# Other product orders in an exact-product feed-forward kernel, and five weight signs on another engine

## The chip, the cores and the metric

The kernel runs on one core of one Trainium2 chip. The time is the device time of one execution in microseconds (us). The engines that matter are TensorE (PE, its weight loads PEld), VectorE (DVE), ScalarE (ACT) and the DMA queue of SyncE (SP).

## What is computed

Attention within chunks of 64 positions, and then a feed-forward layer with a rational activation on its output. The inputs are 8 x 8 heads of 576 positions of 64 elements (float32); the two weight matrices come as float64.

```
scores = q_c @ k_c^T / 8                # per chunk of 64
attn   = exp(scores - max) / (sum + 1e-9)
x      = (attn @ v_c) as (4608, 512)
h = x @ w_in                            # (4608, 2048)
P = a0 + a1 h + a2 h^2 + a3 h^3
Q = 1 + |b0| |h| + |b1| h^2
out = (P / (Q + 1e-6)) @ w_out          # (4608, 512)
```

## The kernel before

**Products in parts.** A float32 product is made from three faster ones of a reduced type. Each operand is split into a high and a low part (`xhi`, `xlo`, `wi_hi`, `wi_lo`, `wo_hi`, `wo_lo`, `ghi`, `glo`), and hi x hi, hi x lo and lo x hi are added up in PSUM.

**Blocks and steps.** The 4608 tokens are 18 blocks of 256 (`NB`, `BT`), and the 2048 middle columns are four stages of 512 (`NST`). A step g is one block n and one stage s. `ff1` (L318) writes `ph`, two PSUM banks that hold 4 groups `fi` of 128 middle columns by 256 tokens: for each `fi` 4 input chunks `cc` times 3 products, 48 matmuls of 256 columns in a step, in two parts (`F`, `f`). Weights are the stationary operand and tokens the moving one. Then a chain of 12 elementwise operations (`chain_a` to `chain_glo`, L331 to L378) on ACT and DVE makes `ghi` and `glo`. `ff2` (L381) adds into `po` (two banks of 512 output columns, `i` for each half of 128 tokens): parts `Z` and `z` use `ghi` with `wo_hi` and `wo_lo`, part `y` uses `glo` with `wo_hi`. Here the tokens are stationary and the output columns moving. A product is 256 columns wide, two (`c`) for each pair of operands, except the four of a block that open and close its sums in the two banks, which are 512 wide (L390 to L392). `ff2` runs two steps behind `ff1` (`LAG`).

**Order of the work.** Nothing is scheduled by a tool. The ramp is a list written out by hand (`START`, L33): each letter is one function and the number its step, block or piece. From step 12 (block 3) on a loop (L464) issues for each step `F f`, the chain and `Z z y` of the step two before, with the attention of the next block between them: scores (`pss`) in stage 0, transposes (`pst`) in stage 1, attention times v (`psx`) in stage 2. The engines run in the order of this text, and semaphores hold an instruction until what it needs is there.

**Weights.** They come in 16 pieces of 128 x 1024 float64 words, loaded by SP into the three `raw` buffers (L143) and turned into float32 during the ramp. `o` (L154, DVE) shifts the low words down by 29; `s` (L158, ACT) scales the high words as float32; `i` (L162, ACT) copies the scaled high words as float16 into the upper half of the low words, where only the sign is left of them; `j` (L166, DVE) shifts the high words and joins both; `h` (L169, ACT) makes the high part and `d` (L174, DVE) the low part. Some pieces take `r` and `l` instead of `d` (PE and ACT). In `START`, the signs of pieces 9, 12, 13 and 10 come between the chains of steps 1 to 4, that of 14 in the chain of step 5, that of 15 in the chain of step 7. The ones that the change touches stand in the text as `G0 w12 i9 g1`, `p2 y1 i12 w10 o13 P2`, `F4 i13 g2 h12 j13`, `T2 i14 Q5` and `g7 i15 H7`.

Of the kernel before, what the change touches and what calls it, by code (L numbers as in the profile page):

```python
# [13 lines left out]
ALU = mybir.AluOpType  # L14
# [7 lines left out]
NHP = 4  # L22
NQ = UPB * NHP
DM = 512
DFF = 2048
FPS = 4
NST = DFF // (128 * FPS)
W = FPS * BT
LAG = 2
# [16 lines left out]
)  # L46
FIRST = 12
PL_TAG = {0: "po", 1: "p1"}

# [4 lines left out]
def tile_chunked_attention_rational_moe(  # L54
# [11 lines left out]
    nc = tc.nc  # L66
# [8 lines left out]
    wi_hi = cp.tile([P, NHP, DFF], F32R, tag="wi_hi", name="wi_hi")  # L75
    wi_lo = cp.tile([P, NHP, DFF], F32R, tag="wi_lo", name="wi_lo")
    wo_hi = cp.tile([P, 16, DM], F32R, tag="wo_hi", name="wo_hi")
    wo_lo = cp.tile([P, 16, DM], F32R, tag="wo_lo", name="wo_lo")
# [8 lines left out]
    def bank_pair(tag, name):  # L87
        return ps.tile([P, 2, 512], F32, tag=tag, name=name)
# [4 lines left out]
    def load_qk(n, early=False):  # L93
        if n >= NB:
            return
        if early:
            q, k = (p2.tile([P, W], F32, tag=t, name=f"{t}qk{n}") for t in "AB")
        else:
            qk = p2.tile([P, 2, W], F32, tag="raw", name=f"qk{n}", bufs=3)
            q, k = qk[:, 0, :], qk[:, 1, :]  # L100
        loaded["q", n], loaded["k", n] = q, k
        if not early:
            load_part(n, slice(0, W))
# [5 lines left out]
    def load_v(n):  # L109
        if n >= NB:  # L110
            return
        v = p2.tile([P, W], F32, tag="vt", name=f"v{n}")
        nc.sync.dma_start(out=v, in_=vP[n])
        loaded["v", n] = v
# [6 lines left out]
    raws, pls = {}, {}  # L121
# [23 lines left out]
    def words(j):  # L145
        low, high = raws[j][:, :, 0], raws[j][:, :, 1]
        return low, high, high.bitcast(F32)
# [10 lines left out]
        nc.scalar.activation(val, val, AF.Copy, scale=2.0 ** -111)  # L158

    def w_sign(j):  # L160
        upper = raws[j].bitcast(mybir.dt.float16).rearrange("p f (w h) -> p f w h", h=2)[:, :, 0, 1]
        nc.scalar.copy(upper, words(j)[2])  # L162

    def w_join(j):
        low, high, val = words(j)
# [150 lines left out]
    ch, gbuf, obuf = {}, {}, {}  # L316

    def ff1(n, s, tag, part):  # L318
        xhi, xlo = xbuf[n]
        if part == 0:  # L320
            ch[n, s] = [bank_pair(tag, f"ph{n}_{s}").rearrange("p a (b t) -> p (a b) t", t=BT), None, None, None]
        ph = ch[n, s][0]
        for fi in range(2 * part, 2 * part + 2):
            f = slice((FPS * s + fi) * P, (FPS * s + fi + 1) * P)
            mm = []
            for cc in range(NHP):
                mm += [(wi_hi, xhi, cc), (wi_hi, xlo, cc), (wi_lo, xhi, cc)]
            for k, (w, x, cc) in enumerate(mm):
                nc.tensor.matmul(ph[:, fi, :], w[:, cc, f], x[:, cc, :], start=(k == 0), stop=(k == len(mm) - 1))  # L329

    def chain_a(n, s):  # L331
        t = lambda tag, bufs: p2.tile([P, FPS, BT], F32, tag=tag, name=f"{tag}{n}_{s}", bufs=bufs)
# [46 lines left out]


    def ff2(n, s, tag, part):  # L381
        if s == 0 and part == 0:
            obuf[n] = bank_pair(tag, f"po{n}")
        ghi, glo = gbuf[n, s]
        if part < 2:
            mm = [(ghi, w, fi, i) for fi in (2 * part, 2 * part + 1) for i in range(2) for w in (wo_hi, wo_lo)]
        else:
            mm = [(glo, wo_hi, fi, i) for i in range(2) for fi in range(FPS)]
        for k, (g, w, fi, i) in enumerate(mm):
            start = s == 0 and part == 0 and k in (0, 2)  # L390
            stop = s == NST - 1 and part == 2 and k in (3, 7)
            for c in ([slice(0, DM)] if start or stop else [slice(0, 256), slice(256, DM)]):  # L392
                nc.tensor.matmul(  # L393
                    obuf[n][:, i, c], g[:, fi, i * 128:(i + 1) * 128], w[:, FPS * s + fi, c], start=start, stop=stop,
                )

    def store(n, last=False):

        rows = out[n * BT:(n + 1) * BT, :].rearrange("(u c t) f -> c u t f", u=UPB, c=2)
        o = p2.tile([P, 2, DM], F32, tag="eo", name=f"o{n}")  # L400
        po = obuf.pop(n)
        if last:
            nc.scalar.copy(o[:, 0, :], po[:, 0, :])
            nc.vector.tensor_copy(o[:, 1, :], po[:, 1, :])
        else:
            nc.scalar.copy(o, po)
        for c in range(2):
            for u in range(UPB):
                nc.sync.dma_start(out=rows[c, u], in_=o[64 * u:64 * u + 64, c, :])
# [22 lines left out]
    def qk(n, u=None):  # L432
# [6 lines left out]
    do = {  # L439
        "k": consts, "B": abs_b1, "q": qk, "v": load_v, "w": w_load,  # L440
        "o": w_low, "s": w_scale, "j": w_join, "i": w_sign, "h": w_hi, "d": w_lo_dve, "r": w_rest, "l": w_lo,
        "S": att_s, "M": att_max, "U": att_sub, "E": att_exp, "n": att_rs, "N": att_norm,
        "T": att_t, "K": att_copy, "A": att_av, "X": att_xhi, "Y": att_xlo,
        "O": store,
    }
    for k, letter in enumerate("Ff"):
        do[letter] = lambda g, k=k: ff1(*steps[g], ph_tag(g), k)
    for k, letter in enumerate("Zzy"):
        do[letter] = lambda g, k=k: ff2(*steps[g], po_tag(steps[g][0]), k)
# [6 lines left out]
    def run(program):  # L456
        for item in program.split():
            do[item[0]](*map(int, item[1:].split(".")))
# [4 lines left out]
    total = len(steps)  # L463
    for g in range(FIRST, total + LAG):  # L464
        n, s = steps[min(g, total - 1)]
        m, stage = n + 1, s if n + 1 < NB and g < total else None
        one = lambda letters, k: run(" ".join(f"{x}{k}" for x in letters))
        if g < total:
            one("Ffab", g)
            if stage == 1:  # L470
                one("nN", m)
            one("cQ", g)
            if stage == 0:
                one("SMU", m)
                load_qk(m + 1)
            if stage == 2:
                one("A", m)
                load_v(m + 1)
            one("IJpP", g)
            if stage == 0:  # L480
                one("E", m)
            if stage == 2:
                one("X", m)
            one("gHRG", g)
            if stage == 2:
                one("Y", m)
        back = steps[g - LAG]
        one("Zzy", g - LAG)
        if back[1] == NST - 1:
            store(back[0], last=(back[0] == NB - 1))  # L490
        if stage == 1:
            one("TK", m)
# [32 lines left out]
```

## Time and profile before

| | us |
|---|---|
| median of 3 runs | 931.86 |
| lowest, highest | 931.72, 932.29 |
| profiled execution | 930.22 |
| its span, first to last instruction | 928.4 |
| PE busy | 886.0 |
| DVE busy | 746.9 |
| ACT busy | 593.9 |

Busy times are sums over the whole span, which is made of a ramp of about 169 us and a steady part. PE's matmuls are pipelined, so that a matmul of 256 columns lasts some 280 ns in the trace while the next one starts long before its end; a rate is read from the distance of the starts, or from the pieces of the chain of waits, and not from the durations.

### The profile page before, as it was taken

The numbers are of one execution on the slowest core, as the hardware profiler recorded it, in microseconds if no ns is written. First come the engines' busy times: TensorE is split into PE (matmuls) and PEld (weight loads), VectorE is DVE, ScalarE is ACT, GpSimd is POOL, SyncE is SP. The second block draws the span as 40 slices with busy tenths as digits, with TensorE's granted clock in tenths as the row PEclk, the third lists the DMA queues.
The fourth block names the chain that finished last, engine by engine and source line by source line (L and its number), as shares of the span: only waits on it lengthen the run. The fifth ranks groups of instructions, "written<-read, shape, count | busy, mean of one in ns | idle before, by whom it ended". The sixth has DMA issues, their size and how long they took to land.

```text
span 928.4 us, 20908 instructions
## 1 busy us (share of the span) xinstructions
PE 886.0 (95%) x9306; PEld 867.7 (93%) x9306; DVE 746.9 (80%) x668; ACT 593.9 (64%) x984; POOL 0.8 (0%) x8
## 2 busy tenths in 40 slices
PE   3589899999999999999999999999999999999997
PEld 2578899999999999999999999999999999999997
DVE  5788888798787878787878787878787888878774
ACT  5999688757474747475757575656565656565452
POOL 0000000000000000000000000000000000000000
PEclk9779899999999999999999999999999999999999
DMA  8443531202020202011110202020202020101011
GB/s 295 165 152 137 181 117 44 55 16 92 1 92 1 86 7 63 30 38 55 24 70 10 83 1 92 2 92 1 92 2 92 2 92 2 47 1 24 1 24 23
DMA packets 20601, 55.87 MB, mean 60 GB/s; under 512 B 2592, under 2 KB 2592, under 8 KB 20512
## 3 DMA queue, kind: packets, MB, share of 16 engines
q1 hardware_dynamic: 20512, 54.54, 18.1%
q8 instruction: 73, 1.20, 0.5%
q14 instruction: 16, 0.13, 0.0%
HBM read 45.09 MB, written 9.44 MB: 59 GB/s over the span
## 4 chain that ended last, share of the span: by engine, by line
PE 82%; ACT 12%; DVE 3%; DMA 2%; issue 1%; SPq 0%; ACTq 0%
PE po L393 39%; PE ph L329 38%; ACT raw L162 3%; PE psx L203 2%; DMA raw<-in_w_in 2%; PE pss L203 2%; ACT raw L158 1%; PE pst L282 1%; ACT e L258 1%; ACT wo_hi L169 1%; ACT A L334 1%; ACT A L349 1%; ACT C L341 1%; ACT B L337 1%; ACT A L353 1%
## 5 line engine op out<-in xcount | busy, mean ns | idle before, releaser
L329 PE MATMUL ph<-xhi,wi_hi 128*128 128x256 f32 x1152 | 326.2, 283 | 8.6 <-DVE C L361 5.2
L329 PE MATMUL ph<-xlo,wi_hi 128*128 128x256 f32 x1152 | 324.2, 281 | 1.6 <-DVE xlo L313 1.6
L329 PE MATMUL ph<-xhi,wi_lo 128*128 128x256 f32 x1152 | 323.6, 281 | 0.0
L334 ACT ACTIVATE A<-ph,ab 128x1024 f32<-128x1024 f32 x72 | 81.3, 1129 | 273.7 <-PE ph L329 272.0
L393 PE MATMUL po<-wo_hi,ghi 128*128 128x256 f32 (+1 forms) x1116 | 230.6, 285 | 3.2 <-DVE ghi L366 3.2
L329 PEld LDWEIGHTS ph<-xhi,wi_hi 128*128 128x128 f32 x1152 | 221.5, 192 | 10.1 <-issue 4.1
L393 PE MATMUL po<-wo_lo,ghi 128*128 128x256 f32 x1152 | 227.5, 279 | 0.0
L329 PEld LDWEIGHTS ph<-xlo,wi_hi 128*128 128x128 f32 x1152 | 219.3, 190 | 2.3 <-DVE xlo L313 2.2
L329 PEld LDWEIGHTS ph<-xhi,wi_lo 128*128 128x128 f32 x1152 | 219.5, 191 | 0.0
L345 DVE SCALAR_TENSOR_TENSOR B<-B,ab,A 128x1024 f32<-128x1024 f32 x72 | 92.4, 1284 | 112.9 <-ACT B L337 112.9
L393 PEld LDWEIGHTS po<-wo_lo,ghi 128*128 128x128 f32 x1152 | 177.9, 188 | 1.6
L393 PEld LDWEIGHTS po<-wo_hi,ghi 128*128 128x128 f32 x1116 | 171.1, 188 | 5.7 <-DVE ghi L366 3.4
L393 PE MATMUL po<-wo_hi,glo 128*128 128x256 f32 (+1 forms) x1116 | 146.9, 284 | 1.9 <-DVE glo L378 1.9
L393 PEld LDWEIGHTS po<-wo_hi,glo 128*128 128x128 f32 x1116 | 137.2, 189 | 3.2 <-DVE glo L378 2.4
L366 DVE SCALAR_TENSOR_TENSOR ghi<-C,ab,A 128x1024 fp32r<-128x1024 f32 x72 | 92.4, 1284 | 11.0 <-ACT A L353 2.4
L349 ACT ACTIVATE A<-B,cst 128x1024 f32<-128x1024 f32 x72 | 83.9, 1166 | 26.4 <-DVE B L345 26.3
L361 DVE SCALAR_TENSOR_TENSOR C<-C,ab,ph 128x1024 f32<-128x1024 f32 x72 | 92.2, 1280 | 3.2 <-ACT B L337 1.0
L374 DVE SCALAR_TENSOR_TENSOR B<-C,ab,B 128x1024 f32<-128x1024 f32 x72 | 92.5, 1285 | 2.4
L378 DVE TENSOR_TENSOR glo<-B,A 128x1024 fp32r<-128x1024 f32 x72 | 88.2, 1225 | 6.8
L357 DVE TENSOR_TENSOR C<-C,ph 128x1024 f32<-128x1024 f32 x72 | 87.5, 1215 | 4.5 <-ACT B L337 3.6
L370 DVE SCALAR_TENSOR_TENSOR B<-B,ghi 128x1024 f32<-128x1024 f32 x72 | 88.2, 1225 | 2.3
L341 ACT ACTIVATE C<-ph,ab 128x1024 f32<-128x1024 f32 x72 | 88.0, 1222 | 2.5 <-DVE B L374 2.3
(53 smaller groups left out, 712.4 us busy)
## 6 DMA issues: line engine op xcount, KB each, us to landing
v<-in_vP SPq DMA_DIRECT2D x18, 512.0 KB, 4.0
out<-o SPq DMA_DIRECT2D x72, 128.0 KB, 2.4
raw<-in_w_in SPq DMA_DIRECT2D x8, 1024.0 KB, 6.6
raw<-in_w_out SPq DMA_DIRECT2D x8, 1024.0 KB, 5.9
qk<-in_qT SPq DMA_DIRECT2D x16, 512.0 KB, 4.7
qk<-in_kT SPq DMA_DIRECT2D x16, 512.0 KB, 5.7
Aqk<-in_qT SPq DMA_DIRECT2D x2, 256.0 KB, 3.4
Bqk<-in_kT SPq DMA_DIRECT2D x2, 256.0 KB, 4.0
```

The lines of the kernel that those rows point to most:

```text
L329: nc.tensor.matmul(ph[:, fi, :], w[:, cc, f], x[:, cc, :], start=(k == 0), stop=(k == len(mm) - 1))
L334: nc.scalar.activation(ch[n, s][1], ch[n, s][0], AF.Abs, scale=b0)
L341: nc.scalar.activation(ch[n, s][3], ch[n, s][0], AF.Identity, bias=a2, scale=a3)
L345: nc.vector.scalar_tensor_tensor(B, B, b1a, A, ALU.mult, ALU.add)
L349: nc.scalar.activation(A, B, AF.Ln, bias=cst[:, 0:1], scale=2.0 ** -KLN)
L357: nc.vector.tensor_mul(C, C, h)
L361: nc.vector.scalar_tensor_tensor(C, C, a1, h, ALU.add, ALU.mult)
L366: nc.vector.scalar_tensor_tensor(gbuf[n, s][0], C, a0, A, ALU.add, ALU.mult)
L370: nc.vector.scalar_tensor_tensor(B, B, CQ, gbuf[n, s][0].bitcast(F32), ALU.add, ALU.mult)
L374: nc.vector.scalar_tensor_tensor(B, C, a0, B, ALU.add, ALU.subtract)
L378: nc.vector.tensor_mul(gbuf[n, s][1], B, A)
L393: nc.tensor.matmul(obuf[n][:, i, c], g[:, fi, i * 128:(i + 1) * 128], w[:, FPS * s + fi, c], start=start, stop=stop,)
```

## The change

1. `ff2` has no 512-column products any more. All are two of 256, also those that open and close a sum; the opening flag is on the first product into each bank and the closing one on the last.
2. Twelve blocks use other orders of the same products (`FORM`). In `ff1`: blocks 4 and 5 put the two products with `xhi` behind each other ("moving"); 6 and 7 run all chunks of one kind of product before the next kind ("kinds"); 8 and 9 alternate between the two PSUM banks with every product and issue all 48 in part `F` ("banks"). In `ff2`: blocks 10 and 11 run all of the first 256 output columns in a part, then the second ("columns"); 12 and 13 all of one half of the tokens, then the other ("chunks"); 14 and 15 run `Z y z`, so that the `glo` products come before the second half of the `ghi` ones ("last").
3. The sign of pieces 9, 12 and 14 is made on DVE by a 16-bit AND of the high word's upper half with 0x8000 into the low word's upper half; that of 13 and 15 by a DVE copy from float32 to float16. The other eleven stay on ACT. The place in the list is the same.

```diff
+FORM = {4: "moving", 5: "moving", 6: "kinds", 7: "kinds", 8: "banks", 9: "banks", 10: "columns", 11: "columns"}
+FORM.update({12: "chunks", 13: "chunks", 14: "last", 15: "last"})
+SIGN_BITS = (9, 12, 14)
+SIGN_ZERO = (13, 15)
...
     def w_sign(j):
-        upper = raws[j].bitcast(mybir.dt.float16).rearrange("p f (w h) -> p f w h", h=2)[:, :, 0, 1]
-        nc.scalar.copy(upper, words(j)[2])
+        halves = raws[j].bitcast(mybir.dt.uint16).rearrange("p f (w h) -> p f w h", h=2)[:, :, :, 1]
+        upper = halves[:, :, 0].bitcast(mybir.dt.float16)
+        if j in SIGN_BITS:
+            nc.vector.tensor_scalar(halves[:, :, 0], halves[:, :, 1], 0x8000, None, ALU.bitwise_and)
+        elif j in SIGN_ZERO:
+            nc.vector.tensor_copy(upper, words(j)[2])
+        else:
+            nc.scalar.copy(upper, words(j)[2])
...
     def ff1(n, s, tag, part):
...
-        for fi in range(2 * part, 2 * part + 2):
+        pairs = [(wi_hi, xhi), (wi_hi, xlo), (wi_lo, xhi)]
+        if form == "moving":
+            pairs = [(wi_hi, xhi), (wi_lo, xhi), (wi_hi, xlo)]
+        mm = [(w, x, cc) for cc in range(NHP) for w, x in pairs]
+        if form == "kinds":
+            mm = [(w, x, cc) for w, x in pairs for cc in range(NHP)]
+        todo = [(fi, k) for fi in (2 * part, 2 * part + 1) for k in range(len(mm))]
+        if form == "banks":
+            todo = [(fi, k) for p in range(2) for k in range(len(mm)) for fi in (p, p + 2)] if part == 0 else []
...
     def ff2(n, s, tag, part):
...
-            mm = [(ghi, w, fi, i) for fi in (2 * part, 2 * part + 1) for i in range(2) for w in (wo_hi, wo_lo)]
+            mm = [(ghi, w, fi, i, c) for fi in (2 * part, 2 * part + 1) for i in range(2) for w in (wo_hi, wo_lo) for c in cs]
         else:
-            mm = [(glo, wo_hi, fi, i) for i in range(2) for fi in range(FPS)]
-        for k, (g, w, fi, i) in enumerate(mm):
-            start = s == 0 and part == 0 and k in (0, 2)
-            stop = s == NST - 1 and part == 2 and k in (3, 7)
-            for c in ([slice(0, DM)] if start or stop else [slice(0, 256), slice(256, DM)]):
+            mm = [(glo, wo_hi, fi, i, c) for i in range(2) for fi in range(FPS) for c in cs]
+        if form == "columns":
+            mm.sort(key=lambda m: m[4])
+        if form == "chunks":
+            mm.sort(key=lambda m: m[3])
+        final = part == (1 if form == "last" else 2)
+        for k, (g, w, fi, i, c) in enumerate(mm):
+            start = s == 0 and part == 0 and (i not in [m[3] for m in mm[:k]])
+            stop = s == NST - 1 and final and (i not in [m[3] for m in mm[k + 1:]])
+            c = slice(256 * c, 256 * c + 256)
...
-        one("Zzy", g - LAG)
+        one("Zyz" if FORM.get(back[0]) == "last" else "Zzy", g - LAG)
```

## Rows read from the trace of the kernel before

**Rows 1.** The page: the span, and PE's busy time with its share of the span and its matmuls (only the beginning of the line is about PE's matmuls; PEld is weight loads).

```profile
span 928.4 us, 20908 instructions
...
PE 886.0 (95%) x9306; PEld 867.7 (93%) x9306; DVE 746.9 (80%) x668; ACT 593.9 (64%) x984; POOL 0.8 (0%) x8
```

**Rows 2.** The windows, busy time of each engine in a stretch. Columns: the stretch and its length in us, busy time (and instructions) of PE, PEld, DVE, ACT and POOL, the granted TensorE clock as a share of 2.4 GHz, the mean busy share of the DMA engines, GB/s.

```profile
94.10:97.70 3.60, 3.55 (x16) 3.32 (x16) 1.50 (x2) 2.06 (x3) 0.00 (x0) 0.54 0.77 284
...
99.90:107.10 7.20, 7.15 (x49) 7.18 (x50) 7.07 (x7) 2.33 (x2) 0.00 (x0) 0.76 0.62 185
...
240.00:863.00 623.00, 623.00 (x6716) 615.12 (x6715) 505.28 (x442) 380.84 (x717) 0.00 (x0) 1.00 0.13 41
```

**Rows 3.** The waits between 170 and 928 us, the longest of all engines: who waited for whom, us in total, how often, the longest.

```profile
ACT A L334 <- PE ph L329: 265.8, 61, 5.8
```

**Rows 4.** The chain of waits in the first part, in order of time: start in us, us on the chain, what.

```profile
90.73 2.58 ACT raw L162
...
124.79 2.49 ACT raw L162
...
142.14 2.60 ACT raw L162
```

**Rows 5.** The timeline of PE in the first part: the instructions ahead of which it waited. Start in us, duration in us, instruction; in brackets the idle time before it and what ended it.

```profile
82.89 0.39 PE L329 MATMUL ph<-xhi,wi_hi 128*128 128x256 f32 x1 [0.55 <-DVE C L361]
...
94.15 3.62 PE L393 MATMUL po<-wo_hi,glo 128*128 128x256 f32 x16 [1.91 <-DVE glo L378]
99.95 0.36 PE L329 MATMUL ph<-xhi,wi_hi 128*128 128x256 f32 x1 [2.18 <-DVE C L361]
```

**Rows 6.** The chain of waits at 196 to 209 us and over one block of tokens at 388 to 436 us; columns as in rows 4, with the number of matmuls (x46 where two matmuls of 512 columns stand for four of 256).

```profile
196.50 5.45 PE ph L329 x48
203.05 5.85 PE po L393 x48
208.89 5.66 PE ph L329 x48
...
388.00 5.65 PE ph L329 x48
394.74 5.64 PE po L393 x48
400.39 5.66 PE ph L329 x48
406.04 5.66 PE po L393 x46
412.57 5.46 PE ph L329 x48
419.13 5.85 PE po L393 x46
424.98 5.46 PE ph L329 x48
430.43 5.44 PE po L393 x48
```

**Rows 7.** The timeline of ACT around one sign copy (L162) and the scale (L158) that follows it; columns as in rows 5.

```profile
80.38 2.91 ACT L162 CAST raw<-raw 128x1024 f16<-128x1024 f32 x1
82.64 1.60 ACT L158 ACTIVATE raw<-raw 128x1024 f32<-128x1024 f32 x1
```

**Rows 8.** The timeline of DVE between 66 and 104 us: joins (L166), shifts (L154) and chain steps; columns as in rows 5.

```profile
72.95 1.23 DVE L166 SCALAR_TENSOR_TENSOR raw<-raw 128x1024 int32<-128x1024 int32 x1 [0.98 <-ACT raw L162]
...
75.63 1.28 DVE L345 SCALAR_TENSOR_TENSOR B<-B,ab,A 128x1024 f32<-128x1024 f32 x1 [0.32 <-ACT B L337]
...
78.03 0.69 DVE L154 TENSOR_SCALAR raw<-raw 128x1024 int32<-128x1024 int32 x1
78.63 1.22 DVE L378 TENSOR_TENSOR glo<-B,A 128x1024 fp32r<-128x1024 f32 x1
...
83.33 1.23 DVE L166 SCALAR_TENSOR_TENSOR raw<-raw 128x1024 int32<-128x1024 int32 x1 [0.49 <-ACT raw L162]
...
87.67 1.23 DVE L166 SCALAR_TENSOR_TENSOR raw<-raw 128x1024 int32<-128x1024 int32 x1 [1.92 <-ACT raw L162]
...
96.20 1.22 DVE L357 TENSOR_TENSOR C<-C,ph 128x1024 f32<-128x1024 f32 x1 [2.10 <-ACT B L337]
```

**Rows 9.** The timeline of DVE between 119 and 155 us; columns as in rows 5.

```profile
127.16 1.28 DVE L361 SCALAR_TENSOR_TENSOR C<-C,ab,ph 128x1024 f32<-128x1024 f32 x1
...
144.77 1.23 DVE L166 SCALAR_TENSOR_TENSOR raw<-raw 128x1024 int32<-128x1024 int32 x1 [0.60 <-ACT raw L162]
...
152.82 1.28 DVE L361 SCALAR_TENSOR_TENSOR C<-C,ab,ph 128x1024 f32<-128x1024 f32 x1 [0.96 <-ACT B L337]
```

**Rows 10.** The timeline of the SP queue: the issue of the load of weight piece 10.

```profile
80.36 0.37 SPq L143 DMA_DIRECT2D raw<-in_w_in  x1
```

**Rows 11.** The DMA issues between 60 and 170 us: the loads of pieces of w_in; count, KB each, median us from issue to landing.

```profile
raw<-in_w_in SPq DMA_DIRECT2D x2, 1024.0 KB, 5.4
```

**Rows 12.** The timeline of PE at the start of an ff2 stretch with 512-column products; columns as in rows 5.

```profile
419.63 0.39 PE L393 MATMUL po<-wo_hi,ghi 128*128 128x512 f32 x1
419.86 0.40 PE L393 MATMUL po<-wo_lo,ghi 128*128 128x256 f32 x2
```

**Rows 13.** The page's costliest groups: weight loads of ff2 on PE; count, busy us, mean ns of one, idle time before them.

```profile
L393 PEld LDWEIGHTS po<-wo_lo,ghi 128*128 128x128 f32 x1152 | 177.9, 188 | 1.6
```

More of the change, by code (lines that the diff above doesn't have):

```diff
@@ L319, in ff1 @@
         xhi, xlo = xbuf[n]
+        form = FORM.get(n, "")
         if part == 0:
@@ L322, in ff1 @@
         ph = ch[n, s][0]
-        for fi in range(2 * part, 2 * part + 2):
-            f = slice((FPS * s + fi) * P, (FPS * s + fi + 1) * P)
[L325 to L329, printed above, removed]
+        pairs = [(wi_hi, xhi), (wi_hi, xlo), (wi_lo, xhi)]
[7 more added lines that the diff above has]
+            todo = [(fi, k) for p in range(2) for k in range(len(mm)) for fi in (p, p + 2)] if part == 0 else []
+        for fi, k in todo:
+            w, x, cc = mm[k]
+            f = slice((FPS * s + fi) * P, (FPS * s + fi + 1) * P)
+            nc.tensor.matmul(ph[:, fi, :], w[:, cc, f], x[:, cc, :], start=(k == 0), stop=(k == len(mm) - 1))
     def chain_a(n, s):
@@ L381, in ff2 @@
     def ff2(n, s, tag, part):
+        form = FORM.get(n, "")
         if s == 0 and part == 0:
@@ L384, in ff2 @@
         ghi, glo = gbuf[n, s]
+        cs = (0, 1)
         if part < 2:
-            mm = [(ghi, w, fi, i) for fi in (2 * part, 2 * part + 1) for i in range(2) for w in (wo_hi, wo_lo)]
+            mm = [(ghi, w, fi, i, c) for fi in (2 * part, 2 * part + 1) for i in range(2) for w in (wo_hi, wo_lo) for c in cs]
         else:
-            mm = [(glo, wo_hi, fi, i) for i in range(2) for fi in range(FPS)]
-        for k, (g, w, fi, i) in enumerate(mm):
-            start = s == 0 and part == 0 and k in (0, 2)
-            stop = s == NST - 1 and part == 2 and k in (3, 7)
-            for c in ([slice(0, DM)] if start or stop else [slice(0, 256), slice(256, DM)]):
-                nc.tensor.matmul(
-                    obuf[n][:, i, c], g[:, fi, i * 128:(i + 1) * 128], w[:, FPS * s + fi, c], start=start, stop=stop,
-                )
+            mm = [(glo, wo_hi, fi, i, c) for i in range(2) for fi in range(FPS) for c in cs]
[8 more added lines that the diff above has]
+            c = slice(256 * c, 256 * c + 256)
+            nc.tensor.matmul(
+                obuf[n][:, i, c], g[:, fi, i * 128:(i + 1) * 128], w[:, FPS * s + fi, c], start=start, stop=stop,
+            )
     def store(n, last=False):
```

## The prediction

> **What bounds the kernel now.** I read the page first: PE is busy for 95% of the 928.4 us span [rows 1]. In the windows by stage, PE is busy 623.00 of 623.00 us between 240 and 863 at granted clock 1.00, while VectorE (DVE) and ScalarE (ACT) leave a fifth and two fifths idle [rows 2]; there ACT's largest wait is for PE (265.8 us) and PE has no wait at all [rows 3]. So two stages have different limits: the ramp, up to about 169 us, where the chain of waits runs through ACT and DVE, and the steady part, where only PE's own pace counts.
>
> In the ramp, the chain of waits passes through ACT's sign copies (L162), about 2.5 us each [rows 4]. PE's own waits there are for DVE: 0.55 us before 82.89, 1.91 before 94.15, 2.18 before 99.95 [rows 5]. The last two have a second price: 94.1 to 97.7 ran at granted clock 0.54 and 99.9 to 107.1 at 0.76, so mostly and partly at 1.2 instead of 2.4 GHz [rows 2].
>
> In the steady part, the chain lists one block of tokens as eight stretches of ff1 (ph) and ff2 (po) [rows 6]. Two paces show: 48 matmuls take 5.45 us (113.5 ns each) or 5.66 us (117.9 ns each). The pace holds for a whole stretch and changes only at its ends; both kinds occur in ph and in po, with the clock at 1.00. A po behind the small attention products carries 0.2 us for its start, so that 5.64 is fast there and 5.85 slow. Of a block's eight, four are slow (ph at 388.00 and 400.39, po at 406.04 and 419.13). One stretch more or less at the slow pace is 48 x 4.4 ns = 0.21 us. This is the only thing that I find in the steady part that an order could change.
>
> **The signs on VectorE.** Pieces 9, 12, 13, 14 and 15 change engine. What ACT loses: one sign holds it 2.26 us (80.38 to the next start at 82.64) [rows 7]. What DVE gains is not in the trace. The nearest row is the shift (L154) of the same raw tile with the same 8-byte step on DVE: it takes 0.69 us, and the next operation starts after 0.60 (78.03 to 78.63) [rows 8]. The bounds are half of that, 0.3, since a 2-byte element is half a word, and above it DVE's other operations on 1024 elements, 1.2 us (127.16 and its like take 1.28) [rows 9], and ACT's 2.26 for this very write. I take 0.60, the row with the same engine, tile, step and one source; nothing speaks for less.
>
> With 0.60, followed along both queues:
> - Piece 9: DVE does the sign itself instead of waiting 0.98 us for ACT before its join at 72.95, and the 0.32 us wait for ACT before 75.63 goes as well [rows 8]: DVE is 0.9 us ahead after it. Behind the sign on DVE stand L366, the join and the L345 for which ACT's L349 waits; all come earlier.
> - Piece 12: 0.60 of that lead is paid ahead of the L361 for which PE waits before 82.89, so PE starts 0.3 earlier. The join at 83.33 loses its 0.49 us wait, the one at 87.67 its 1.92 us wait, for one more sign of 0.60 (piece 13) [rows 8].
> - ACT, rid of three signs, is held by the load of piece 10, issued at 80.36 behind PE's release [rows 10] and landing some 5.4 us later [rows 11], and by DVE's shift of piece 10. That piece's sign stays on ACT (90.73 in rows 4) and starts near 88.5. So DVE's L357 at 96.20, whose wait of 2.10 us is for ACT [rows 8], starts at 94.0, and PE's ph of 99.95 at 97.75: 2.2 us.
> - PE's po products of 94.15 start 2.1 us earlier and at full clock, but then PE idles 3.8 us before 97.75. A stretch with 2.2 us of idleness ahead of it ran partly at 1.2 GHz, so I expect that again behind 97.75: nothing gained, nothing lost.
> - Piece 14: ACT drops 2.5 us (124.79 in rows 4), DVE pays 0.60 ahead of the L361 at 127.16. Piece 15: DVE's 0.60 us wait at 144.77 goes, 0.60 is paid. The L361 at 152.82, for which PE waits next, is 2.2 us earlier [rows 9], and this reaches the saturated part at 169.
>
> Sum: **-2.2 us**. At 1.2 us a sign, the lead at 96.20 shrinks to 0.7, piece 14 eats it and the ramp ends 0.5 us later. At 2.26, PE starts 82.89 about 3 us late and piece 14 adds 2 more: +6. DVE has no other cover there than its waits in rows 8 and 9. At 0.3 the lead is held by the load of piece 10: -3. The SP queue keeps its order; a load that waits for a raw buffer is released earlier, none later at 0.60.
>
> **No 512-column products.** 72 of them become 144 of 256. After a 512-column one the next product starts 0.23 us later (419.63 to 419.86) [rows 12]; two of 256 take 0.227 at the fast pace, 0.236 at the slow. So 72 x (-0.003 to +0.006): -0.2 to +0.4 us; I take 0. Each split adds a weight load of 188 ns [rows 13], which the pace of 113.5 ns shows to be hidden. The Trainium skill (TensorE: Matmul & The Clock Gate, section "Back-to-back issue gap") speaks against the split: a sustained stream gives about 131 ns for a product of 512 columns and 81 ns for one of 128. By that, an estimate from that page, a pair of narrow ones costs at least 162 ns and 72 splits at least 2.2 us more. The row, 0.23 us for a wide one, contradicts it, and the row decides.
>
> **The other orders.** ph changes in blocks 4 to 9, po in 10 to 15. Default ph holds, side by side, pairs that share weights and pairs that share nothing, twelve products in a row into one place; default po holds runs of four and of two with the same weights and a change of bank after every four. All go at either pace [rows 6], so the order itself is priced at 0. Blocks 14 and 15 use glo 16 products (1.8 us) earlier; ff2 runs two steps behind its chain, and PE shows no wait at all after 170. The bounds are the paces: all eight stretches fast in the 16 blocks of the main loop is 16 x 4 x 0.21 = -13.4 us, all slow +13.4.
>
> On the pace without the 512s: the po at 419.13 begins with two of them, and the ph behind it is fast (424.98). At 203.05 a po of 48 narrow products, also behind the small attention products, is slow, and the ph behind it is slow too (208.89) [rows 6]. If the first becomes like the second, ph at 424.98 turns slow, po at 430.43 with it (a po keeps the pace of the ph ahead of it, as at 400.39 and 406.04), and the ph after that (388.00 in this block) fast; the po of 394.74, which then has a fast ph ahead of the attention products, as the po of 203.05 had (196.50), turns slow too. Three turn slow and one fast: two more slow stretches a block, 0.42 us. I take this for the four blocks whose products keep their order (2, 3, 16, 17): **+1.7 us**. For the twelve others I know no rule and take as many slow as now: 0.
>
> **Sum.** -2.2 + 0 + 1.7 + 0 = -0.5 us. The profiled execution took 930.22 (span 928.4 and 1.8 around it); the median, 931.86, lies 1.6 above it, which I take as unchanged. Forecast 931.4 us. A measurement of this kernel tells about 0.2%, 1.9 us, from no change.
>
> **Rivals.**
> - *The ramp's gain stays whole* (927 to 929.7): the signs are fast, and no pace or rather fewer stretches are lost, -2.2 to -5. For: by rows 6 half the stretches are slow for nothing that looks like data. Against: the stretch at 203.05. Chance 0.26.
> - *The slow pace spreads* (slower, 936.4): two more slow stretches in all 16 blocks, 16 x 0.42 = +6.7, less 2.2. It decides once three of the six reordered pairs behave like the default order (each pair 0.84, total +2.0). For: a pace changes only at a stretch's end, and the products at the ends are of the same kinds in most orders. Against: only one stretch without 512s to read it from. Chance 0.22.
> - *VectorE does not take the signs at the shift's rate* (the change does not do what it says): at 1.2 us +0.5 + 1.7, 934.1; at 2.26 +6 + 1.7, 939.6. For: ACT takes 2.91 us over this write and 1.60 over the 4-byte scale of such a tile [rows 7]. It decides above 1.15 us a sign. Chance 0.21.
> - *The added weight loads show*: 188 - 113 = 75 ns each at most, x 72 = +5.4, 936.8. The rule of the Trainium skill named above points this way. Against: every product of 256 has its load, and none shows. Chance 0.03.
> - *Forecast*: 0.28.
>
> **How the numbers follow.** Faster, 0.28: the first rival and the forecast's edge (0.02). Slower, 0.40: the second, the fourth, 0.13 of the third and 0.02 of the forecast. Within 0.2%, 0.32: the rest of the forecast, and of the third rival where only one of the two ways is slow. The range 926.5 to 939.0 takes in the first rival, the second, the fourth and the third short of its far end; it leaves out paces far from today's and two losses at once.
>
> **What will show it.** Right: sign rows on DVE of 0.69 us with the next start after 0.60; the 1.92 us wait before a join gone; PE's ph of 99.95 near 97.7 and its last wait in the ramp 2 us earlier; in blocks 4 to 15 only stretches of 5.45 or 5.66 us. Wrong: a third pace in some block, which would give an order a price of its own; sign rows of 1.2 us or more; slow stretches per block far from four to six.

## The result, and the profile after

The changed kernel takes 938.19 us (median of 5 runs, 935.76 to 938.75) beside 931.72 (930.10 to 932.29): ratio 1.0065, interval 1.0046 to 1.0085. It is 6.5 us slower. The forecast was 931.4; the time lies inside the range, near its upper end, and on the side that had the chance of 0.40. That it lies inside is luck: two losses came at once, which the prediction says that its range leaves out.

The page of the kernel after, first the span, then busy times [rows 1]:

```profile
span 936.7 us, 21044 instructions
...
PE 892.0 (95%) x9378; PEld 877.2 (94%) x9378; DVE 751.8 (80%) x673; ACT 582.8 (62%) x979; POOL 0.8 (0%) x8
```

PE has 72 more matmuls and is busy 6.0 us longer, at the same share of the span. The window of the steady part [rows 2] has PE busy throughout, and at full clock, as before:

```profile
240.00:863.00 623.00, 623.00 (x6723) 617.96 (x6722) 500.74 (x440) 379.48 (x715) 0.00 (x0) 1.00 0.13 41
```

So neither a wait nor the clock took the time there. The chain of waits over one block shows what did [rows 6] (ff1 is now L347, ff2 L418):

```profile
386.77 5.65 PE po L418 x48
392.42 5.45 PE ph L347 x48
...
398.96 5.85 PE po L418 x48
404.81 5.66 PE ph L347 x48
410.47 5.66 PE po L418 x48
...
416.99 5.46 PE ph L347 x48
...
423.54 5.85 PE po L418 x48
429.39 5.66 PE ph L347 x48
435.05 1.06 PE po L418 x9
```

Only the paces of before occur, but six stretches of eight are slow instead of four: fast are the ph at 392.42 and at 416.99. A block takes 435.05 - 386.77 = 48.28 us; before it was 430.43 + 5.44 - 388.00 = 47.87. The same cycle stands in all blocks, whatever their order of products. Counted from the distances between matmul starts, some 3620 narrow (256-column) products between 240 and 866 us go at 117.8 ns; before it was some 2328. The difference, 1292 x 4.4 ns, is 5.7 us.

In the ramp, the lines by form show the signs on both engines (L169 the AND and L171 the copy on DVE, L173 the rest on ACT), and the timeline of DVE shows two of them and what follows [rows 8]:

```profile
L173 ACT CAST raw<-raw 128x1024 f16<-128x1024 f32 x11 | 28.8, 2616 | 0.7 <-DVE raw L159 0.6
...
L169 DVE TENSOR_SCALAR raw<-raw 128x1024 uint16<-128x1024 uint16 x3 | 4.0, 1348 | 0.0
L171 DVE CAST raw<-raw 128x1024 f16<-128x1024 f32 x2 | 2.7, 1342 | 0.0
```

```profile
81.92 1.37 DVE L169 TENSOR_SCALAR raw<-raw 128x1024 uint16<-128x1024 uint16 x1
83.06 0.76 DVE L159 TENSOR_SCALAR raw<-raw 128x1024 int32<-128x1024 int32 x1
...
84.90 1.23 DVE L177 SCALAR_TENSOR_TENSOR raw<-raw 128x1024 int32<-128x1024 int32 x1
86.03 1.35 DVE L171 CAST raw<-raw 128x1024 f16<-128x1024 f32 x1
87.16 1.27 DVE L384 SCALAR_TENSOR_TENSOR ghi<-C,ab,A 128x1024 fp32r<-128x1024 f32 x1
```

A sign holds DVE 1.14 us (81.92 to 83.06) or 1.13 (86.03 to 87.16), either way, where the prediction had 0.60. The four waits for ACT before joins (L177) that the prediction named, 4.0 us together, are gone, as predicted, but five signs at 1.14 us take 5.7 us of DVE.

### The profile page after: what moved, and what is told of

It is laid out like the page before. It is cut to its first block, busy times and chain, and to the rows that moved or that the text cites. A ratio compares the mean times of both kernels' runs of the same rounds, so it can differ in the third digit from the quotient of the medians.

```text
span 936.7 us, 21044 instructions
## 1 busy us (share of the span) xinstructions
PE 892.0 (95%) x9378; PEld 877.2 (94%) x9378; DVE 751.8 (80%) x673; ACT 582.8 (62%) x979; POOL 0.8 (0%) x8
## 4 chain that ended last, share of the span: by engine, by line
PE 82%; ACT 8%; DVE 5%; DMA 2%; issue 2%; SPq 1%; ACTq 0%
PE po L418 39%; PE ph L347 38%; ACT raw L173 2%; PE psx L214 2%; PE pss L214 2%; DMA raw<-in_w_in 1%; PE pst L293 1%; ACT e L269 1%; ACT raw L163 1%; DVE C L375 1%; ACT A L352 1%; DVE C L379 1%; ACT C L359 1%; DVE B L363 1%; ACT B L355 1%
## 5 line engine op out<-in xcount | busy, mean ns | idle before, releaser
L347 PE MATMUL ph<-xhi,wi_hi 128*128 128x256 f32 x1152 | 300.6, 284 | 11.2 <-DVE C L379 7.6
L347 PE MATMUL ph<-xlo,wi_hi 128*128 128x256 f32 x1152 | 298.4, 282 | 1.6 <-DVE xlo L324 1.6
L347 PE MATMUL ph<-xhi,wi_lo 128*128 128x256 f32 x1152 | 297.9, 281 | 0.0
L418 PE MATMUL po<-wo_hi,ghi 128*128 128x256 f32 x1152 | 237.9, 283 | 4.1 <-DVE ghi L384 4.1
L418 PE MATMUL po<-wo_lo,ghi 128*128 128x256 f32 x1152 | 234.4, 280 | 0.0
L347 PEld LDWEIGHTS ph<-xhi,wi_hi 128*128 128x128 f32 x1152 | 210.1, 192 | 12.5 <-issue 6.5
L347 PEld LDWEIGHTS ph<-xlo,wi_hi 128*128 128x128 f32 x1152 | 208.4, 191 | 2.2 <-DVE xlo L324 2.2
L347 PEld LDWEIGHTS ph<-xhi,wi_lo 128*128 128x128 f32 x1152 | 208.2, 191 | 0.0
L418 PEld LDWEIGHTS po<-wo_hi,ghi 128*128 128x128 f32 x1152 | 181.2, 189 | 6.6 <-DVE ghi L384 4.3
L418 PEld LDWEIGHTS po<-wo_lo,ghi 128*128 128x128 f32 x1152 | 181.1, 189 | 0.0
L418 PE MATMUL po<-wo_hi,glo 128*128 128x256 f32 x1152 | 147.1, 279 | 0.4 <-DVE glo L396 0.4
L418 PEld LDWEIGHTS po<-wo_hi,glo 128*128 128x128 f32 x1152 | 140.5, 188 | 0.9 <-DVE glo L396 0.6
```

Of the source, the lines that this page charges most:

```text
L418: nc.tensor.matmul(obuf[n][:, i, c], g[:, fi, i * 128:(i + 1) * 128], w[:, FPS * s + fi, c], start=start, stop=stop,)
```

## The experiments

Each kernel is compared with the kernel before on the same chip. Theory A: without the 512-column ("wide") products the stretches fall into another cycle of the two paces; the orders and the signs matter little. Rivals: the orders cost it (B), or the signs do (C).

**The parts, one at a time.** The split alone:

```diff
-            for c in ([slice(0, DM)] if start or stop else [slice(0, 256), slice(256, DM)]):
+            for h in range(2):
+                c = slice(256 * h, 256 * h + 256)
```

> The kernel before with one edit: the 72 products of 512 columns are two of 256 each; all orders as before, all signs on ACT. Theory A (the wide products alone set the paces): six of the eight stretches of every block are slow, 3620 slow products between 240 and 866 us instead of 2328, and the time is 6.5 us above the kernel before (938.3 beside 931.7). Rival B (the other orders cost it): four of eight stay slow, time within 1 us of before. Rival C (the signs on DVE cost the ramp 3 us, the products the other 3.4): 3.4 us above before.

Measured: 936.25 beside 930.62, ratio 1.0062 (1.0049 to 1.0074): +5.6 us, with 3620 slow products, as many as in the changed kernel. With the default orders alone the steady part is as slow as the changed one.

The other orders alone, the first and last product of each bank wide as before:

```diff
+            c = slice(0, DM) if k in opens + ends else slice(256 * c, 256 * c + 256)
```

> The changed kernel's orders in blocks 4 to 15, with the first and the last product of each output bank at 512 columns again, all signs on ACT. Theory A: four of eight stretches slow in every block whatever its order, time within 1 us of the kernel before. Rival B: six of eight slow in the blocks with other orders, 12 x 0.41 = 5 us above before. Rival C: as before.

Measured: 932.27, ratio 1.0015 (1.0006 to 1.0024): +1.65 us, with 2700 slow products, 372 more than before, x 4.4 ns = 1.6 us. They lie in blocks 10 to 13 (4 x 2 stretches x 48 = 384). The chain of this kernel, first in a block whose ff1 has the other order, then in one of the order "columns":

```profile
323.48 5.85 PE po L423 x46
329.33 5.46 PE ph L347 x48
334.78 5.44 PE po L423 x48
...
562.85 5.85 PE po L423 x46
568.69 5.66 PE ph L347 x48
574.35 5.65 PE po L423 x48
```

Behind the wide opening at 323.48 the ph is fast, as in the kernel before; behind that at 562.85 it is slow. In the default order two narrow products stand between the two wide ones, in "columns" one, in "chunks" (blocks 12 and 13) six. So B is wrong for four orders of six. In the other two the cycle parts from that of before at one place, the ph behind the opened po. Whether the number of products between the wide ones does it, or the order of the rest of that po, is not shown: in the first map below, one wide product alone or two side by side at that place leave the ph fast.

The signs alone (the change's `w_sign` in the kernel before):

> The kernel before with one edit: the signs of pieces 9, 12, 13, 14 and 15 on DVE. Theory A: the steady part is unchanged, and with 1.26 us a sign on DVE the end of the ramp moves by -1 to +0.5 us; time within 1.5 us of the kernel before. Rival B: the same. Rival C: the ramp ends 3 us later, 934.7.

Measured: 931.45, ratio 1.0010 (1.0001 to 1.0020): +0.8 us. C falls.

The changed kernel with all signs on ACT (`SIGN_BITS = ()`, `SIGN_ZERO = ()`):

> The changed kernel with one part undone: the five signs are on ACT again. Theory A: like the split alone, 6.5 us above the kernel before. Rival B: also about 6.5 above, so that only the two kernels before it tell A from B. Rival C: 3.4 us above.

Measured: 936.99, ratio 1.0063 (1.0050 to 1.0077): +6.4 us. Its steady part is that of the split alone, the same six slow stretches of eight, so the 0.7 us between the two kernels lies elsewhere. Split and signs, 5.6 + 0.8, come to the change's 6.5, but parts below about 1 us are not resolved: taken from this kernel, the signs would be worth 0.1.

**Which wide products.** Only the opening two wide (`if start else`), and only the closing two (`if stop else`):

> The kernel before, with the two closing 512-column products of each block narrow and only the two opening ones wide. Theory A1 (the opening products alone decide, because the po behind the second group of attention products then ends without a fast product): four slow stretches of eight, time within 0.7 us of the kernel before. Rival A2 (each wide product counts, wherever it stands): half of the split's cost, 2.9 us above. Rival A3 (the closing ones decide): 5.7 us above.

> The mirror: the two opening products of each block narrow and only the two closing ones wide. A1: six slow stretches of eight, 5.7 us above the kernel before, as without any wide product. A2: 2.9 us above. A3: within 0.7 us of before.

Measured: openings 930.14 beside 930.68, ratio 0.9994 (0.9985 to 1.0003); closings 936.65, ratio 1.0062 (1.0049 to 1.0075). A1 holds: the openings decide, the closings do nothing. The chain of the kernel with wide closings alone, around the value products (`psx`):

```profile
414.73 5.46 PE ph L329 x48
420.19 1.09 PE psx L203 x64
421.29 5.85 PE po L394 x48
427.13 5.66 PE ph L329 x48
```

This is the place of [rows 6] where a fast ph followed at 424.98. In both kernels the po is slow; behind the one that opens wide the ph is fast, behind the one that opens narrow it is slow.

**Maps of the paces.** Two kernels with another edit in each pair of blocks: wide products at other places of po, and products cut into two of 128. (The first also has piece 9's sign as a 4-byte AND.)

> A map of paces, no time: the kernel before with other sets of 512-column products in the po stretches of each pair of blocks (a stretch has 24 such pairs of narrow ones): 2 and 3 all 24; 4 and 5 the opening two places (0 and 2) in all four stretches; 6 and 7 place 0; 8 and 9 the last; 10 and 11 the last two; 12 and 13 the first two; 14 and 15 the middle one; 16 and 17 the closing places (19 and 23), the last five of these in all four stretches as well. If the pace is set at the start of a stretch, only sets with place 0 differ from the cycle of two fast in eight; if any 512-column product can shift it, the middle one changes the pace inside a stretch. Piece 9's sign is taken by a 4-byte AND on DVE that writes over the low word (its three low mantissa bits are left out): 0.69 us if the 2-byte write makes the changed kernel's signs long, 1.3 us if reading one word and writing another does.

> A map of paces, no time: the kernel before, with a product cut into two of 128 columns at one place in each pair of blocks: 2 and 3 the first product of every ph stretch; 4 and 5 its last; 6 and 7 the first of its second half; 8 and 9 its first two; 12 and 13 the first of each quarter; 14 and 15 the last of every po stretch; 16 and 17 the first of it. In 10 and 11 nothing is cut, but the score products of the next block go ahead of the ph stretch instead of behind it. If the pace is decided at the start of a stretch, the cuts at the ends of ph change which stretches are slow and the others don't; if some set leaves fewer than four of eight slow, a kernel faster than both can be made from it, 3.3 us for each stretch of a block. If the pace has nothing to do with the products at the ends, all stay at four of eight.

In the first map (one run, 927.52), blocks 10 and 11, whose po stretches end with two wide pairs (pairs of narrow products made one wide product each), have six fast stretches and take 47.50 us; the other sets took 47.6 to 48.1. Its chain there, in time order, `x46` for 44 narrow and two wide products:

```profile
561.83 5.85 PE po L400 x46
567.68 5.46 PE ph L335 x48
573.14 5.45 PE po L400 x46
578.59 5.46 PE ph L335 x48
584.05 1.09 PE pss L209 x64
585.14 5.85 PE po L400 x46
590.99 5.46 PE ph L335 x48
596.46 5.45 PE po L400 x46
601.90 0.87 PE pst L288 x8
602.77 5.46 PE ph L335 x48
```

Every ph behind such an end is fast, also behind a fast po, where before it was slow (400.39 behind 394.74 [rows 6]). Slow remain the two po's behind the small attention products. A wide pair in the middle of a fast po turns the rest of it slow (5.54 us instead of 5.45), so that a pace does not only change at the ends.

In the second map (one run, 940.03) the cuts bring nothing: blocks 2 to 9 and 12 to 15 took 48.1 to 49.5 us each, more than the 47.87 without a cut. But in blocks 10 and 11, where only the score products moved ahead of the ph, that ph and the po behind it were fast.

**Putting it together.** Wide ends in all blocks of the loop, in place of openings and closings:

```diff
+            pieces = [slice(0, DM)] if (start or stop if n < 2 else part == 2 and k > 5) else [slice(0, 256), slice(256, DM)]
```

> The kernel before with its 512-column products elsewhere: in every po stretch of blocks 2 to 17 the last two places (22 and 23) are wide, and none at the opening; blocks 0 and 1 as before. Theory A1 (a stretch's pace is set by what stands at its boundary, whichever the sum of narrow products): as in blocks 10 and 11 of the map of 512-column sets, two slow stretches of eight, 47.50 instead of 47.87 us a block, 16 x 0.37 = 5.9 us faster than the kernel before. Rival A4 (in that map the pace came from the neighbouring blocks' other sets): not two of eight, time within 2 us of before.

Measured: 924.05 beside 930.81, ratio 0.9920 (0.9907 to 0.9934): 6.8 us faster than the kernel before. Its blocks take 47.50 us, with two slow stretches of eight, as expected.

A third map, with the attention products at other places:

> A map of paces: wide ends as in the kernel with the wide last places, and the small attention products elsewhere. The score products of the next block go ahead of the first ph stretch of a block instead of behind it, in all blocks; blocks 4, 5, 14, 15 take the value products in the middle of the third ph stretch; 6, 7, 10 to 13 take the transposes in the middle of the po ahead of it and the value products before it. In 8 and 9 the po ahead of the score products ends narrow, in 10, 11, 14, 15 that of the fourth as well, in 12 and 13 only the last place is wide. If the slow stretches of the wide-ended kernel come from the attention products standing between a fast ph and its po, a set with none there has no slow stretch at all: 47.1 us a block. If attention products turn what follows them slow wherever they stand, two slow stretches remain and only their names change.

In one run (929.48), all eight stretches of blocks 4 and 5 were fast, with the scores ahead of the first ph and the value products in the middle of the third. Where the transposes were moved forward too, PE waited for DVE's normalisation ahead of them, up to 1.6 us each time. Where a po ended narrow and the value products followed in the next ph, slow stretches came back. So that first arrangement was made for all blocks:

```diff
+            if stage == 0:
+                one("S", m)
+            one("F", g)
+            if stage == 2:
+                one("A", m)
+            one("fab", g)
```

> The kernel with the wide last places, and two groups of small attention products moved: the scores of the next block ahead of the first ph stretch of a block, its value products into the middle of the third. Theory A1: as in blocks 4 and 5 of the map of places, no slow stretch, 47.08 us a block instead of 47.87 before: 16 x 0.79 = 12.6 us faster than the kernel before, 918.2 beside 930.8. Rival A5 (two slow ones come back, or PE waits for the attention steps that the moved products need): no faster than the wide-ended kernel, 924.

Measured: 919.41 beside 931.29, ratio 0.9870 (0.9856 to 0.9883): 11.9 us faster than the kernel before and 18.8 below the changed one's median. Its chain over one block:

```profile
386.65 5.64 PE ph L329 x48
392.29 5.45 PE po L394 x46
397.74 5.46 PE ph L329 x48
403.20 5.45 PE po L394 x46
...
409.52 2.74 PE ph L329 x24
412.26 1.09 PE psx L203 x64
413.35 2.94 PE ph L329 x24
416.28 5.45 PE po L394 x46
421.73 5.46 PE ph L329 x48
427.19 5.45 PE po L394 x46
...
433.73 5.64 PE ph L329 x48
```

All are fast (5.64 and 2.94 carry the 0.2 us start behind small products), and a block takes 433.73 - 386.65 = 47.08 us. Less than 4% of the products of 240 to 866 us are slow.

**The price of a sign.** The same five signs as a 4-byte AND:

```diff
+        if j in (9, 12, 13, 14, 15):
+            nc.vector.tensor_scalar(words(j)[0], words(j)[1], -2 ** 31, None, ALU.bitwise_and)
+            return
```

> The kernel before with the same five signs on DVE as in the changed kernel, but each taken by a 4-byte AND that writes over the low word (the three lowest mantissa bits of these five pieces are left out). Theory D1 (the ramp's step of the prediction is right, only the price of a sign was wrong): with 0.69 us a sign the ramp ends 2.2 us earlier, 928.6 beside 930.8, where the 2-byte signs gave +0.9. Theory D2 (the ramp's end hangs on what TensorE's clock does, not on when VectorE hands over): within 1 us of the kernel before.

Measured: 928.86 beside 931.29, ratio 0.9973 (0.9962 to 0.9984): 2.4 us faster. D1 holds. Its signs (line by form), one of them in the timeline of DVE, and PE's ph of 99.95 [rows 5] in the timeline of PE:

```profile
L162 DVE TENSOR_SCALAR raw<-raw 128x1024 int32<-128x1024 int32 x5 | 3.4, 690 | 0.0
```

```profile
80.92 0.69 DVE L162 TENSOR_SCALAR raw<-raw 128x1024 int32<-128x1024 int32 x1
81.52 0.69 DVE L154 TENSOR_SCALAR raw<-raw 128x1024 int32<-128x1024 int32 x1
```

```profile
98.55 0.35 PE L332 MATMUL ph<-xhi,wi_hi 128*128 128x256 f32 x1 [3.67 <-DVE C L364]
```

With the next operation 0.60 us behind a sign (80.92 to 81.52), that ph comes 1.4 us earlier, in an execution whose ff1 of step 1 began 0.97 later (47.98 instead of 47.01): 2.4 us gained in between, and 3.67 us of idleness before it, where the prediction had 3.8.

## Why the prediction was wrong

Two steps failed, and both on the same side. The first missed by 3.9 us (5.6 for the paces instead of 1.7), the second by 3.0 (+0.8 instead of -2.2): together 6.9 of the 7.0 between the forecast change of -0.5 and the measured 6.5.

**"For the twelve others I know no rule and take as many slow as now: 0."** The part about the default order was right, stretch by stretch: the ph behind the opened po turns slow, the po behind it too, the next ph fast, the po behind the scores slow; two more slow ones a block, 0.42 us there, 0.41 measured. The failed step was to stop at the four blocks with that order. The argument rested on what stands at the ends of stretches, and once all products are narrow, no order changes the width of what stands there; it should have been carried to all blocks. The second rival did so: its +6.7 us for the paces is within 1.1 of the 5.6 that the split alone cost (the loop runs over 15 blocks, the prediction counted 16, and the ramp's paces differ from run to run).

**"I take 0.60, the row with the same engine, tile, step and one source; nothing speaks for less."** Something spoke for more: the element written was 2 bytes, and the row was of 4. Measured 1.14 us a sign, next to the 1.2 of the third rival, which gave +0.5 for the ramp; the signs alone cost +0.8. The walk along the queues itself was right: at the assumed price, in the kernel with 4-byte signs, the time falls by 2.4 us where -2.2 stood, and TensorE runs the 7.15 us from 98.55 at a granted clock of 0.76, as it did from 99.90 before. The Trainium skill (VectorE: DVE Perf Modes, section "What auto-detection actually checks") lets an operation with a single source, source and destination in SBUF and their outermost dimensions both even or equal, take two elements a cycle, and names no element size as a condition for it. The 4-byte AND agrees with it, 0.69 us like the shift, beside 1.23 for a join with two sources (84.90 above); the 2-byte AND at the same 8-byte step, 1.35 us, does not, and the measurement decides.

**The rivals were not exclusive.** The second (paces) and the third (sign price) both came true: 931.86 + 6.7 + 0.5 = 939.1, beside 938.19 measured. The prediction gave them chances of 0.22 and 0.21 as if each excluded the other, and took the ramp's gain off in the second.

**Right by the profile:** the split costs nothing by itself (with the 36 closing products split and the openings wide, no difference from before); the added weight loads don't show (the same six-of-eight cycle accounts for the whole cost); no order has a pace of its own. The claim that the pace "changes only at its ends" holds for the stretches of narrow products in the steady part; a wide or cut product inside can change it.

**Not settled:** what in TensorE holds a stretch at 113.3 or 117.8 ns. The runs give rules, not their cause: a po behind a fast ph and small products is slow; a ph behind two wide pairs is fast; with narrow products alone, a ph takes the other pace than the po ahead of it, except behind a slow po that stands after small products, where it is slow too (404.81 behind 398.96 above). Stretches of the first map that open wide do not all fit the last of these. Nor is it settled why the changed kernel's times fall in two groups, 935.8 and 938.2 to 938.8. In the profiled execution, one of the longer, TensorE ran the ramp's 6.8 us from 99.80 at half its clock, where the kernel before had 0.76 in about that stretch [rows 2]. The signs alone do not bring that: in the same stretch the changed kernel with all signs on ACT had 0.54, and the kernel with the signs alone 0.75. The row of the changed kernel:

```profile
99.80:106.60 6.80, 5.96 (x28) 5.99 (x29) 6.71 (x7) 3.07 (x3) 0.00 (x0) 0.50 0.52 161
```

## What to carry to other kernels

When PE is saturated and its matmul starts show two paces, as here, treat the pace as a state that the products at the ends of a stretch may hand on: follow it through the whole cycle of the loop before an edit at such an end is priced, and then look for the ends that leave it fast. Take an operation's duration from a row with the same element size, not only the same engine and step. And before rivals get their chances, ask whether they can come true together.

## What the runs showed of the hardware

- Two wide pairs at the end of each ff2 stretch, in place of a block's wide openings and closings and with no less work, are worth 0.37 us in each 47.87 us block; with two groups of small products moved, 0.79 us, or 1.3% of the kernel's time.
- A po stretch of 24 wide products, in the first map, takes 5.52 us, 230 ns each: between the 5.45 and the 5.66 of 48 narrow ones.

```profile
213.79 5.52 PE po L400 x24
...
238.10 5.51 PE po L400 x24
```

  The 131 ns that the Trainium skill gives (TensorE: Matmul & The Clock Gate, section "Back-to-back issue gap") for a sustained stream of 512 columns is again not what these products show.
- On DVE, a 2-byte element written at an 8-byte step costs 1.35 us for 1024 elements of a partition (read as 2 bytes by the AND, as 4 by the copy), a 4-byte one 0.69, whether AND or shift; on ACT the same 2-byte write takes 2.6 us (above) beside 1.2 for the 4-byte scale in the changed kernel:

```profile
L163 ACT ACTIVATE raw<-raw 128x1024 f32<-128x1024 f32 x16 | 19.6, 1223 | 10.6 <-DMA raw<-in_w_in 9.3 <-DMA raw<-in_w_out 1.3
```
